# Three rounded products in place of one f32 product in the fill of a fused attention and two-layer expert kernel

## Chip, cores and metric

One core of one Trainium2 chip. The metric is the device time of the program in microseconds; three runs of the kernel before give a median of 1349.17 us (1349.16 to 1350.17).

## The reference, cut

```python
f = 1 / (1 + exp(-f_logit))                       # q, k, v, f_logit: (4, 8, 768, 48)
for t in range(768):                              # gated linear attention
    state = f[:, :, t, :, None] * state + k_t v_t^T
    y[:, :, t] = q_t . state
x = y as (3072, 384)
h = x @ w_in                                      # 384 -> 2048
g = (a0 + a1 h + a2 h^2 + a3 h^3) / (1 + |b0||h| + |b1| h^2 + 1e-6)
x = g @ w_out                                     # 2048 -> 384
out = sum over 4 experts e of p_e * (relu(x @ w1[e]) @ w2[e])   # 384 -> 1024 -> 384
```

## The kernel before

The 768 positions are cut into NCH = 6 chunks of 128; a chunk has NB = 4 batches, and a `Block` is one chunk of one batch of the attention (4 pairs of heads side by side). The first feed-forward layer is cut into NJ1 = 16 slots of 128 hidden columns; a slot has an input half (384 columns of `w_in`) and an output half (384 of `w_out`). The experts have 8 slots each.

All engines run instructions in the order in which the program lists them (a manual schedule), so that a waiting instruction holds everything listed behind it on its engine. SP issues nearly all DMAs, also in that order.

Three stretches follow each other.

**Start-up.** `Att.first(s, ...)` runs for rounds s = 0 to 4 (tau = -6 to -2). Round s prepares block (0, s): ScalarE's `exp`, VectorE's `w` (L437, f + 1, clipped), four `scans` (L444), ScalarE's `inverse` (L452, L453), `k_hat` (L458, GpSimd but for the first block), `newton1`, `newton2` and `q_hat` (L464, L468, L473), then its scores on TensorE. The same round ends the block before it (`old`): `k_copy`, `masked` (L488), products for y, and `x_hi` (L553), which copies the block's y from a bank to the tile `x` of chunk 0. In chunk 0, x is one f32 tile and `x_lo` does nothing. Between them stand conversions of the first slots: the slots of the first layer come as 64-bit words and `conv` makes f32 of them (L805, L806 on ScalarE, L808, L809 on VectorE, L812 an integer add, on VectorE for the first four slots and on GpSimd for the others). VectorE's list in rounds 1 and 2 is: w, scans, masked, newton1, newton2, q_hat, L808, L809, L812. ScalarE's in round 1: inverse, k_copy, L805, L806, exp of the next block, x_hi; in round 2 the exp stands ahead of L805.

**Fill.** Steps tau = 0 to 17 take chunk 0 through the first layer. Step tau has `fill_in(tau + 1)` (three f32 products, L961) and `fill_out(tau - 2)` (three f32 products, L969). An f32 product stands in the trace as two MATMUL records. `gate_step` makes the rational function between them: on VectorE L993, L1002 and L1012 of the slot before and L998, L1004 and L1019 of the new one, on ScalarE L982 to L984, L999 and L1000. The conversion of a later slot follows (L808, L809, then L812 on GpSimd). In steps tau = 0 to 3 `scale_state` (L581, two GpSimd products of 48 partitions) stands ahead of that step's L812. Each converted slot is stored whole to DRAM (`w1s`), to be used again for the chunks after.

**Main part.** From step v = -1 (v = tau - 19) the experts of chunk c run while chunk c + 1 goes through attention and the first layer. These products are "rounded": each f32 operand is split in a high part in fp32r and a low part, and three fp32r products (L910, L920) stand for one. A slot's half that is used for the first time is loaded raw, its high part made by ScalarE (L865), its low part by GpSimd or VectorE (L867), and if it is used again, both parts are stored (`scr`); from then on it is loaded split. For the 16 input halves of the first layer this first use is in steps v = 10 to 26, and the splits run about eight uses ahead. Block (1, 0) has its `q_hat` on GpSimd at the end of step v = -2.

Of the kernel before, what the change touches and what calls it, by code (L numbers as in the profile page):

```python
# [8 lines left out]
F32 = mybir.dt.float32  # L9
# [10 lines left out]
C = 128  # L20
# [386 lines left out]
class Block:  # L407
# [25 lines left out]
    def w(self):  # L433
        f = d = self.f[0:PR]
        if self.c > 1:
            d = self.d = self.py[0:PR].rearrange("p (r t) -> p r t", r=NP)
        self.nc.vector.tensor_scalar(d, f, 1.0, WLIM, ALU.add, ALU.min)  # L437

    def scans(self):
        self.g = self.att.p1.tile([128, NP, C], F32, tag="g", name="g")  # L440
# [28 lines left out]

    def q_hat(self):  # L470
        q = self.q[0:PR]
        eng = self.nc.gpsimd if self.c else self.nc.vector
        eng.tensor_tensor(out=q, in0=q, in1=self.i[0:PR], op=ALU.mult)  # L473

    def scores(self, r):
# [68 lines left out]
        self.nc.tensor.matmul(self.pa[0:PR, o:o + 2 * D], self.kt[:, r], self.v[:, o:o + 2 * D], start=True, stop=True)  # L544

    def x_part(self, i):
        x = self.att.x_of(self.c)
        x = x if self.c == 0 else x[:, i]
        return x[:, :, self.b * C:(self.b + 1) * C]

    def x_hi(self):
        xt = self.py[:, 0:DM].rearrange("p (m t) -> p m t", m=3)
        self.nc.scalar.copy(out=self.x_part(0), in_=xt)  # L553

    def x_lo(self):
        if self.c:
            xt = self.py[:, 0:DM].rearrange("p (m t) -> p m t", m=3)
            self.nc.vector.tensor_tensor(out=self.x_part(1), in0=xt, in1=self.x_part(0).bitcast(F32), op=ALU.subtract)

    def finish(self):  # L560
        nc = self.nc
# [22 lines left out]
class Att:  # L584
# [9 lines left out]

    def x_of(self, c):
        if c not in self.x:
            shape, dt = ([128, 3, 512], F32) if c == 0 else ([128, 2, 3, 512], F32R)
            self.x[c] = self.xp.tile(shape, dt, tag="x", name="x")
        return self.x[c]

    @staticmethod
# [21 lines left out]
        for _ in range(n):  # L623
            self.tc.nc.tensor.matmul(self.spare[:, 0:C], ident, ident, start=True, stop=True)

    def first(self, s, conv, fetch, ahead):

        new, old, nxt = (self.blocks.get((0, b)) for b in (s, s - 1, s + 1))
        rs = range(NP)
        if s == 0:  # L630
            new.exp()
            self.warm(WARM[0])
        if new:
            new.w()
            new.scans()
            new.inverse()
            new.k_hat()
        if s == 0:
            self.scalars()
        if old:  # L640
            old.k_copy()
        if nxt and s != 1:
            nxt.exp()
        for f in conv[0]:
            f()
        if s == 1:
            nxt.exp()
        if old:
            old.masked()
            for f in old.y_parts():  # L650
                f()
            for r in rs:
                old.update(r)
        if new:
            new.newton1()
            new.newton2()
            new.q_hat()
        if old:
            old.x_hi()
        if new:  # L660
            self.warm(WARM[1])
            for r in rs:
                new.scores(r)
            for r in rs:
                new.k_t(r)
            if nxt:
                self.warm(WARM[2 + s])
            else:
                ahead()
        if old:  # L670
# [45 lines left out]
    def early(self, blk, v):  # L716

        s = {}
        if blk.b == 0:
            s = {-4: {ACT0: [blk.exp]}, -3: {POST: [blk.w, blk.scans]},  # L720
                 -2: {POST: [blk.inverse, blk.k_hat, blk.newton1, blk.newton2, blk.q_hat]},
                 0: {PB: [blk.all_scores], REST: [blk.masked]},
                 1: {PB: 5 * [lambda: None] + [blk.keys_and_y] + 3 * [lambda: None], REST: [blk.k_copy, blk.x_hi]},
                 2: {PA: 4 * [lambda: None] + [blk.all_updates] + 4 * [lambda: None], DVE1: [blk.x_lo, blk.finish]}}
        if blk.b == 1:
            s = {-1: {ACT0: [blk.exp]}, 0: {DVE1: [blk.w], REST: [blk.scans]},
                 1: {ACT0: [blk.inverse], POOL1: [blk.k_hat], REST: [blk.newton1, blk.newton2, blk.q_hat]},
                 2: {REST: [blk.all_scores]}, 3: {**self.stage(blk, 5), DVE1: [blk.masked]},
                 4: {**self.stage(blk, 6), DVE1: [blk.x_lo, blk.finish], REST: []}}
        if blk.b == 2:  # L730
            s = {1: {ACT0: [blk.exp]}, 2: {DVE1: [blk.w], REST: [blk.scans]},
                 3: {ACT0: [blk.inverse], POOL1: [blk.k_hat], DVE1: [blk.newton1], REST: [blk.newton2, blk.q_hat]},
                 5: self.stage(blk, 5), 6: self.stage(blk, 6)}
            s[4], s[5] = {REST: [blk.all_scores]}, {**s[5], DVE1: [blk.masked]}
        return s.get(v, {})
# [17 lines left out]
def fused(ctx, tc, aps, consts, gm, big, dp, prep, flag_op):  # L753
# [18 lines left out]
    att.scalars = prep.scalars  # L772
    att.e0 = tp.tile([128, NB, NP], F32, tag="t", name="e0")

    w1s = [dp.tile([128, SW], F32, name=f"w1s{j}") for j in range(NJ1)]
    scr = {(i, h): dp.tile([128, 2, DM], F32, name=f"ws{i}_{h}") for i in range(NSLOT) for h in range(2)}
    prs = dp.tile([NCH * NB * NE, C], F32, name="prs")

# [16 lines left out]
    def conv(i, stage):  # L795
        if stage == 0:
            t = spare_pools[i % 3].tile([128, 2 * SW], F32, tag=("o", "s1", "pb")[i % 3], name="t")
            temp[i] = t
        f = temp[i]
        p, m = f[:, 0:SW], f[:, SW:2 * SW].bitcast(I32)  # L800
        pi = p.bitcast(I32)
        words = raw[i].rearrange("p (n w) -> p n w", w=2)
        lo, hi = words[:, :, 0], words[:, :, 1]
        if stage == 0:
            nc.scalar.activation(out=p, in_=hi.bitcast(F32), func=AF.Abs, scale=2.0 ** -112, accum_out=big[:, i:i + 1])  # L805
            nc.scalar.activation(out=m, in_=lo.bitcast(U32), func=AF.Identity, scale=2.0 ** -29)  # L806
        else:
            nc.vector.tensor_scalar(pi, pi, 3, None, ALU.logical_shift_left)  # L808
            nc.vector.scalar_tensor_tensor(out=pi, in0=hi, scalar=-2 ** 31, in1=pi, op0=ALU.bitwise_and, op1=ALU.bitwise_or)  # L809
            w1f[i] = wp.tile([128, SW], F32, tag="w", name="wf")  # L810
            eng = nc.vector if CONV1[i] < NB - 6 else nc.gpsimd
            eng.tensor_tensor(out=w1f[i].bitcast(I32), in0=pi, in1=m, op=ALU.add)  # L812
            late.append(partial(nc.sync.dma_start, out=w1s[i], in_=w1f[i]))
            if i % 2:
                late.append(fetch)

    late = []

# [16 lines left out]
    state = {"ready": 0, "split": 0, "used": 0, "vec": False}  # L835
    tile_of, raw_of, stores, seen = {}, {}, [], set()
    rawbuf = []
    again = {h for n, h in enumerate(uses) if h in uses[:n]}
    first_use = [h not in uses[:n] for n, h in enumerate(uses)]

    def make_ready(n):
        while state["ready"] < min(n, len(uses)):
            k = state["ready"]
            state["ready"] += 1
            i, h = uses[k]
            t = tile_of[k] = wp.tile([128, 2, DM], F32R, tag="w", name="w")
# [273 lines left out]
    for v in range(-FILL - 6, LAST + 1):  # L1120
# [282 lines left out]
```

## Time and profile before

| | |
|---|---|
| median of 3 runs | 1349.17 us |
| the profiled execution | 1348.14 us, of which span 1346.3 us |
| TensorE (PE) busy | 1322.1 us, 98% of the span |
| VectorE (DVE) busy | 906.0 us, 67% |
| ScalarE (ACT) busy | 666.2 us, 49% |
| GpSimd (POOL) busy | 280.3 us, 21% |
| mean granted TensorE clock | 0.998 |

The span runs from the first to the last instruction; 1.84 us of the profiled execution lie outside it. A busy share is a mean over stretches that have different limits, and the ends of matmuls are modelled, so that TensorE's share says little by itself. In a timeline a row has its start, its time, engine, line, operation, output<-inputs, and, in brackets, how long the engine sat idle before it and what released it. Rows of one line that follow each other are merged (x2, x4).

### The profile page before, as it was taken

Reading aid. Unit: us, or ns where it says so; the run is one execution under the profiler, and the core shown is the slowest. Engines: PE = TensorE matmul, PEld = TensorE weight load, DVE = VectorE, ACT = ScalarE, POOL = GpSimd, SP = SyncE. Lnnn points to the kernel's source line nnn. Section 1 sums busy time; section 2 is a strip of 40 time slices with the busy share of each in tenths; the row PEclk is TensorE's granted clock in tenths of the full one; section 3 lists DMA queues with packets and bytes.
Section 4 is the critical chain, followed back from the end, with each engine's and each line's share of the span. In section 5 each row is a group of like instructions: output and inputs, shape, how many; then the busy total and the mean of one; then the engine's idle time right before and its main releaser. Section 6 shows DMA issues by size and latency. Waiting matters only on the chain.

```text
span 1346.3 us, 19626 instructions
## 1 busy us (share of the span) xinstructions
PE 1322.1 (98%) x7180; PEld 1058.6 (79%) x7180; DVE 906.0 (67%) x1389; ACT 666.2 (49%) x1164; POOL 280.3 (21%) x235
## 2 busy tenths in 40 slices
PE   8998999999999999999999999999999999999998
PEld 7444888778788888888888888888888888888887
DVE  8999868998566776757665947676856565752221
ACT  5996557757355545445444525454535544421111
POOL 2333334576310122100120220010210010110010
PEclk9999999999999999999999999999999999999999
DMA  9638985767785665676666657666757666667660
GB/s 348 210 143 315 368 311 203 275 237 260 278 273 177 196 213 176 198 243 206 200 212 182 213 183 256 218 191 195 220 179 239 193 196 191 195 192 241 192 194 27
DMA packets 116855, 294.16 MB, mean 219 GB/s; under 512 B 13232, under 2 KB 28944, under 8 KB 115984
## 3 DMA queue, kind: packets, MB, share of 16 engines
q1 hardware_dynamic: 116320, 292.70, 66.8%
q8 instruction: 59, 0.97, 0.3%
q14 instruction: 44, 0.36, 0.1%
q10 hardware_dynamic: 432, 0.13, 0.0%
HBM read 243.98 MB, written 48.81 MB: 217 GB/s over the span
## 4 chain that ended last, share of the span: by engine, by line


## 5 line engine op out<-in xcount | busy, mean ns | idle before, releaser
L910 PE MATMUL bank<-x,w 128*128 128x512 f32 x2448 | 595.2, 392 | 5.7 <-DVE gl L1033 4.9
L910 PEld LDWEIGHTS bank<-x,w 128*128 128x128 f32 x2448 | 458.2, 188 | 103.7 <-DVE gl L1033 6.6
L920 PE MATMUL bank<-gh,w 128*128 128x512 f32 x1584 | 492.6, 392 | 0.8 <-DVE s L1091 0.8
L920 PEld LDWEIGHTS bank<-gh,w 128*128 128x128 f32 x1584 | 294.1, 188 | 66.4 <-issue 4.0
L920 PE MATMUL bank<-gl,w 128*128 128x512 f32 x792 | 308.6, 390 | 0.0
L1033 DVE SCALAR_TENSOR_TENSOR gl<-bank,gh 128x512 fp32r<-128x512 f32 x192 | 131.6, 685 | 136.1 <-ACT gh L1032 135.7
L1074 POOL TENSOR_TENSOR o<-o,t 128x512 f32<-128x512 f32 x64 | 92.4, 1470 | 535.0 <-DVE t L1067 535.0
L1032 ACT ACTIVATE gh<-bank 128x512 fp32r<-128x512 f32 x192 | 113.9, 594 | 121.1 <-PE bank L910 121.1
L920 PEld LDWEIGHTS bank<-gl,w 128*128 128x128 f32 x792 | 148.7, 188 | 31.2
L998 DVE SCALAR_TENSOR_TENSOR q<-q,sc,r 128x512 f32<-128x512 f32 x80 | 67.0, 837 | 141.5 <-ACT r L983 141.5
L1009 ACT CAST gh<-q 128x512 fp32r<-128x512 f32 x80 | 49.2, 615 | 162.6 <-DVE q L1007 162.5
L978 ACT COPY h<-bank 128x512 f32<-128x512 f32 x80 | 47.0, 588 | 112.9 <-PE bank L910 112.8
L867 POOL TENSOR_TENSOR w<-rawbuf,w 128x384 fp32r<-128x384 f32 x68 | 79.2, 1190 | 33.3 <-ACT w L865 27.4
L1024 DVE TENSOR_TENSOR gl<-q,gh 128x512 fp32r<-128x512 f32 x80 | 56.8, 710 | 32.8 <-ACT gh L1009 32.6
L1019 DVE SCALAR_TENSOR_TENSOR y<-y,sc,h 128x512 f32<-128x512 f32 x80 | 74.9, 936 | 2.8
L999 ACT ACTIVATE r<-q,sc 128x512 f32<-128x512 f32 x80 | 58.0, 725 | 27.3 <-DVE q L998 20.4
L993 DVE SCALAR_TENSOR_TENSOR q<-q,r 128x512 f32<-128x512 f32 x80 | 68.6, 857 | 0.1
L458 POOL TENSOR_TENSOR k<-k,g 112x512 f32<-112x512 f32 x23 | 34.4, 1496 | 153.7 <-DVE g L444 77.2
L984 ACT ACTIVATE y<-h,sc 128x512 f32<-128x512 f32 x80 | 64.2, 802 | 0.0
L1007 DVE SCALAR_TENSOR_TENSOR q<-y,sc,q 128x512 f32<-128x512 f32 x80 | 62.2, 777 | 1.8
L1000 ACT ACTIVATE r<-r 128x512 f32<-128x512 f32 x96 | 60.7, 632 | 3.0
L1091 DVE TENSOR_TENSOR s<-s,bank 128x512 f32<-128x512 f32 x45 | 30.1, 685 | 45.9 <-PE bank L920 45.8
(117 smaller groups left out, 1275.5 us busy)
## 6 DMA issues: line engine op xcount, KB each, us to landing
w<-ws SPq DMA_DIRECT2D x456, 384.0 KB, 3.5
ws<-w SPq DMA_DIRECT2D x96, 384.0 KB, 4.8
raw<-in_w_dram SPq DMA_DIRECT2D x16, 768.0 KB, 6.8
rawbuf<-in_w_dram SPq DMA_DIRECT2D x64, 192.0 KB, 4.8
v<-in_v_dram SPq DMA_DIRECT2D x24, 320.0 KB, 5.1
f<-in_qkf_dram SPq DMA_DIRECT2D x24, 256.0 KB, 3.9
k<-in_qkf_dram SPq DMA_DIRECT2D x24, 256.0 KB, 4.0
q<-in_qkf_dram SPq DMA_DIRECT2D x24, 256.0 KB, 4.5
```

The source lines that it names most:

```text
L867: eng.tensor_tensor(out=t[:, 1], in0=r, in1=t[:, 0].bitcast(F32), op=ALU.subtract)
L910: nc.tensor.matmul(ps, a[:, o], b[:, kk, :], start=(n == 0), stop=(n == 8))
L920: nc.tensor.matmul(acc[m], a[:, o], b, start=(start and n == 0), stop=(stop and n == last))
L984: nc.scalar.activation(out=y, in_=h, func=AF.Identity, scale=sc[:, 0:1], bias=sc[:, 1:2])
L993: vec.scalar_tensor_tensor(out=q0, in0=q0, scalar=QC, in1=r0, op0=ALU.add, op1=ALU.mult)
L998: vec.scalar_tensor_tensor(out=q, in0=q, scalar=sc[:, 5:6], in1=r, op0=ALU.mult, op1=ALU.add)
L1000: nc.scalar.activation(out=r, in_=r, func=AF.Exp, scale=-1.0)
L1007: vec.scalar_tensor_tensor(out=q0, in0=y0, scalar=sc[:, 3:4], in1=q0, op0=ALU.subtract, op1=ALU.mult)
L1019: vec.scalar_tensor_tensor(out=y, in0=y, scalar=sc[:, 2:3], in1=h, op0=ALU.subtract, op1=ALU.mult)
L1032: nc.scalar.activation(out=gh, in_=h, func=AF.Relu)
L1033: nc.vector.scalar_tensor_tensor(out=gl, in0=h, scalar=0.0, in1=gh.bitcast(F32), op0=ALU.max, op1=ALU.subtract)
L1074: add()
```

## The change

The first-layer input products of the fill become three rounded ones. For this the tile x of chunk 0 gets a high and a low part, so that `x_lo` (L558, a VectorE subtraction) now runs for the four blocks of chunk 0; and a new function `split_in(i)` splits the input half of slot i on GpSimd (a copy and a subtraction) and stores both parts. The later uses load the halves split, with no first-use split. Only the output half goes to `w1s`. Besides, `w` moves from VectorE to ScalarE for all 24 blocks, right behind `exp`, and the `q_hat` of block (1, 0) moves from GpSimd to VectorE.

```diff
     def w(self):
-        self.nc.vector.tensor_scalar(d, f, 1.0, WLIM, ALU.add, ALU.min)
+        self.nc.scalar.activation(out=d, in_=f, func=AF.Identity, bias=self.att.consts[0][0:PR, 8:9])
     def q_hat(self):
-        eng = self.nc.gpsimd if self.c else self.nc.vector
+        eng = self.nc.gpsimd if self.c and (self.c, self.b) != (1, 0) else self.nc.vector
     def x_lo(self):
-        if self.c:
-            xt = ...
-            self.nc.vector.tensor_tensor(out=self.x_part(1), in0=xt, in1=self.x_part(0).bitcast(F32), op=ALU.subtract)
+        xt = ...
+        self.nc.vector.tensor_tensor(out=self.x_part(1), in0=xt, in1=self.x_part(0).bitcast(F32), op=ALU.subtract)
     def first(self, s, conv, fetch, ahead, split):
         if s == 0:
             new.exp()
+            new.w()
         if new:
-            new.w()
             new.scans()
...
         if old:
             old.k_copy()
+        if s == NB - 1:
+            split(0)
         if nxt and s != 1:
             nxt.exp()
+            nxt.w()
         for f in conv[0]:
             f()
         if s == 1:
             nxt.exp()
+            nxt.w()
...
         if old:
             old.x_hi()
+            if not nxt:
+                old.x_lo()
...
         if old:
             old.finish()
+            if nxt:
+                old.x_lo()
         for f in conv[1]:
             f()
 # fused
+    def split_in(i):
+        h, l = win[i] = (g2p.tile(..., tag="gh"), g2p.tile(..., tag="gl"))
+        src = w1f[i][:, 0:DM]
+        nc.gpsimd.tensor_copy(out=h[:, 0:DM], in_=src)
+        nc.gpsimd.tensor_tensor(out=l[:, 0:DM], in0=src, in1=h[:, 0:DM].bitcast(F32), op=ALU.subtract)
+        for n, t in enumerate((h, l)):
+            late.append(partial(nc.sync.dma_start, out=scr[i, 0][:, n], in_=t[:, 0:DM].bitcast(F32)))
-    first_use = [h not in uses[:n] for n, h in enumerate(uses)]
+    first_use = [h not in uses[:n] and (h[0] >= NJ1 or h[1]) for n, h in enumerate(uses)]
     def fill_in(j, lo=0, hi=NB):
         for kk in range(3):
-            nc.tensor.matmul(ps[:, t], w[:, kk * 128:(kk + 1) * 128], att.x[0][:, kk, t], start=(kk == 0), stop=(kk == 2))
+            for a, b in ((wh, x[:, 0]), (wl, x[:, 0]), (wh, x[:, 1])):
+                nc.tensor.matmul(ps[:, t], a[:, o], b[:, kk, t], start=(n == 0), stop=(n == 8))
 # main loop, at the head of step tau
+        if 1 <= tau + 3 < NJ1:
+            split_in(tau + 3)
```

## Rows read from the trace of the kernel before

**Rows 1.** The windows: busy us (count) of PE, PEld, DVE, ACT, POOL; then clock, DMA.

```profile
60.00:80.00 20.00, 20.00 (x47) 8.41 (x46) 19.86 (x32) 18.05 (x31) 6.60 (x4) 1.00 0.65 236
...
200.00:300.00 100.00, 96.82 (x552) 78.31 (x551) 93.73 (x121) 69.30 (x127) 57.75 (x46) 1.00 0.68 239
304.00:308.00 4.00, 4.00 (x13) 3.09 (x12) 3.42 (x6) 3.85 (x8) 2.56 (x3) 0.57 1.01 369
1100.00:1120.00 20.00, 20.00 (x90) 16.57 (x89) 12.71 (x17) 6.21 (x11) 4.70 (x3) 1.00 0.60 184
```

**Rows 2.** The timeline of one fill step: start us, us, engine, line, operation.

```profile
59.62 0.75 DVE L998 SCALAR_TENSOR_TENSOR bank<-bank,sc,r 128x512 f32<-128x512 f32 x1
...
62.79 0.55 DVE L808 TENSOR_SCALAR t<-t 128x768 int32<-128x768 int32 x1
...
63.38 0.96 DVE L809 SCALAR_TENSOR_TENSOR t<-raw,t 128x768 int32<-128x768 int32 x1
...
64.48 1.83 POOL L812 TENSOR_TENSOR wf<-t 128x768 int32<-128x768 int32 x1 [3.38 <-DVE t L809]
...
64.86 0.75 DVE L998 SCALAR_TENSOR_TENSOR bank<-bank,sc,r 128x512 f32<-128x512 f32 x1
```

**Rows 3.** The timeline of start-up round 1, VectorE and ScalarE.

```profile
14.28 0.69 DVE L473 TENSOR_TENSOR q<-q,i 112x512 f32<-112x512 f32 x1
...
14.83 0.66 ACT L431 ACTIVATE f<-f 112x512 f32<-112x512 f32 x1
14.89 0.55 DVE L808 TENSOR_SCALAR t<-t 128x768 int32<-128x768 int32 x1
15.35 0.50 ACT L553 COPY x<-bank 128x384 f32<-128x384 f32 x1
```

**Rows 4.** The timeline of start-up rounds 2 and 4 and the first gate.

```profile
22.22 0.69 DVE L473 TENSOR_TENSOR q<-q,i 112x512 f32<-112x512 f32 x1
...
23.44 0.45 ACT L553 COPY x<-bank 128x384 f32<-128x384 f32 x1
...
33.73 1.28 DVE L488 TENSOR_TENSOR am<-bank,mask 128x512 f32<-128x512 f32 x2
...
36.22 0.48 ACT L553 COPY x<-bank 128x384 f32<-128x384 f32 x1 [1.81 <-PE bank L501]
...
39.22 0.76 DVE L998 SCALAR_TENSOR_TENSOR bank<-bank,sc,r 128x512 f32<-128x512 f32 x1 [0.35 <-ACT r L983]
```

**Rows 5.** The groups by line, 0 to 210 us: busy us, mean ns.

```profile
L437 DVE TENSOR_SCALAR f<-f 112x512 f32<-112x512 f32 x8 | 3.9, 488 | 3.4 <-ACT f L431 3.3
...
L558 DVE TENSOR_TENSOR x<-bank,x 128x384 fp32r<-128x384 f32 x4 | 2.2, 547 | 0.0
```

**Rows 6.** The timeline, GpSimd: memsets and subtractions of 384 elements.

```profile
0.73 1.48 POOL L612 MEMSET s<- 128x384 f32 x4 [0.29 <-POOLq L1390]
...
111.28 1.96 POOL L867 TENSOR_TENSOR w<-rawbuf,w 128x384 fp32r<-128x384 f32 x2 [2.40 <-ACT w L865]
```

**Rows 7.** The timeline, GpSimd and VectorE side by side, at 238 us.

```profile
238.37 3.50 DVE L993 SCALAR_TENSOR_TENSOR q<-q,r 128x512 f32<-128x512 f32 x1
238.37 4.37 POOL L867 TENSOR_TENSOR w<-rawbuf,w 128x384 fp32r<-128x384 f32 x4
```

**Rows 8.** The timeline of the q_hat of block (1,0) on GpSimd.

```profile
125.78 2.46 POOL L473 TENSOR_TENSOR q<-q,i 112x512 f32<-112x512 f32 x1 [3.15 <-DVE i L468]
```

**Rows 9.** The waits of TensorE from 122 to 400 us: in all, times, longest.

```profile
PE bank L910 <- DVE gl L1033: 4.9, 3, 1.8
PE bank L477 <- POOL q L473: 1.7, 1, 1.7
PE bank L493 <- DVE am L488: 1.5, 1, 1.5
PE bank L920 <- DVE s L1091: 0.8, 1, 0.8
PE bank L910 <- ACT h L978: 0.8, 1, 0.8
```

More of the change, by code (lines that the diff above doesn't have):

```diff
@@ L546, in x_part @@
     def x_part(self, i):
-        x = self.att.x_of(self.c)
-        x = x if self.c == 0 else x[:, i]
-        return x[:, :, self.b * C:(self.b + 1) * C]
+        return self.att.x_of(self.c)[:, i, :, self.b * C:(self.b + 1) * C]
     def x_hi(self):
@@ L555, in x_lo @@
     def x_lo(self):
-        if self.c:
-            xt = self.py[:, 0:DM].rearrange("p (m t) -> p m t", m=3)
-            self.nc.vector.tensor_tensor(out=self.x_part(1), in0=xt, in1=self.x_part(0).bitcast(F32), op=ALU.subtract)
+        xt = self.py[:, 0:DM].rearrange("p (m t) -> p m t", m=3)
+        self.nc.vector.tensor_tensor(out=self.x_part(1), in0=xt, in1=self.x_part(0).bitcast(F32), op=ALU.subtract)
     def finish(self):
@@ L596, in x_of @@
         if c not in self.x:
-            shape, dt = ([128, 3, 512], F32) if c == 0 else ([128, 2, 3, 512], F32R)
-            self.x[c] = self.xp.tile(shape, dt, tag="x", name="x")
+            self.x[c] = self.xp.tile([128, 2, 3, 512], F32R, tag="x", name="x")
         return self.x[c]
@@ L624, in warm, with first @@
             self.tc.nc.tensor.matmul(self.spare[:, 0:C], ident, ident, start=True, stop=True)
-    def first(self, s, conv, fetch, ahead):
+    def first(self, s, conv, fetch, ahead, split):
         new, old, nxt = (self.blocks.get((0, b)) for b in (s, s - 1, s + 1))
@@ L719, in early @@
         if blk.b == 0:
-            s = {-4: {ACT0: [blk.exp]}, -3: {POST: [blk.w, blk.scans]},
+            s = {-4: {ACT0: [blk.exp, blk.w]}, -3: {POST: [blk.scans]},
                  -2: {POST: [blk.inverse, blk.k_hat, blk.newton1, blk.newton2, blk.q_hat]},
@@ L725, in early @@
         if blk.b == 1:
-            s = {-1: {ACT0: [blk.exp]}, 0: {DVE1: [blk.w], REST: [blk.scans]},
+            s = {-1: {ACT0: [blk.exp, blk.w]}, 0: {REST: [blk.scans]},
                  1: {ACT0: [blk.inverse], POOL1: [blk.k_hat], REST: [blk.newton1, blk.newton2, blk.q_hat]},
@@ L730, in early @@
         if blk.b == 2:
-            s = {1: {ACT0: [blk.exp]}, 2: {DVE1: [blk.w], REST: [blk.scans]},
+            s = {1: {ACT0: [blk.exp, blk.w]}, 2: {REST: [blk.scans]},
                  3: {ACT0: [blk.inverse], POOL1: [blk.k_hat], DVE1: [blk.newton1], REST: [blk.newton2, blk.q_hat]},
@@ L773, in fused @@
     att.e0 = tp.tile([128, NB, NP], F32, tag="t", name="e0")
-    w1s = [dp.tile([128, SW], F32, name=f"w1s{j}") for j in range(NJ1)]
+    w1s = [dp.tile([128, DM], F32, name=f"w1s{j}") for j in range(NJ1)]
     scr = {(i, h): dp.tile([128, 2, DM], F32, name=f"ws{i}_{h}") for i in range(NSLOT) for h in range(2)}
@@ L809, in conv @@
             nc.vector.scalar_tensor_tensor(out=pi, in0=hi, scalar=-2 ** 31, in1=pi, op0=ALU.bitwise_and, op1=ALU.bitwise_or)
+            eng = nc.vector if CONV1[i] < NB - 6 else nc.gpsimd
             w1f[i] = wp.tile([128, SW], F32, tag="w", name="wf")
-            eng = nc.vector if CONV1[i] < NB - 6 else nc.gpsimd
             eng.tensor_tensor(out=w1f[i].bitcast(I32), in0=pi, in1=m, op=ALU.add)
-            late.append(partial(nc.sync.dma_start, out=w1s[i], in_=w1f[i]))
+            late.append(partial(nc.sync.dma_start, out=w1s[i], in_=w1f[i][:, DM:SW]))
             if i % 2:
                 late.append(fetch)
+    win = {}
+    def split_in(i):
+        h, l = win[i] = (g2p.tile([128, 512], F32R, tag="gh", name="gh"), g2p.tile([128, 512], F32R, tag="gl", name="gl"))
+        src = w1f[i][:, 0:DM]
[3 more added lines that the diff above has]
+            late.append(partial(nc.sync.dma_start, out=scr[i, 0][:, n], in_=t[:, 0:DM].bitcast(F32)))
     late = []
@@ L853, in make_ready @@
                 seen.add(k)
-                src = w1s[i] if i < NJ1 else w2[i - NJ1]
-                nc.sync.dma_start(out=r, in_=src[:, h * DM:(h + 1) * DM])
+                src = w1s[i] if i < NJ1 else w2[i - NJ1][:, h * DM:(h + 1) * DM]
+                nc.sync.dma_start(out=r, in_=src)
             else:
@@ L958, in fill_in @@
     def fill_in(j, lo=0, hi=NB):
-        w, ps, t = w1f[j], (banks[3], banks[4], banks[7])[j % 3], slice(lo * C, hi * C)
+        (wh, wl), ps, t = win[j], (banks[3], banks[4], banks[7])[j % 3], slice(lo * C, hi * C)
+        x, n = att.x[0], 0
         for kk in range(3):
-            nc.tensor.matmul(ps[:, t], w[:, kk * 128:(kk + 1) * 128], att.x[0][:, kk, t], start=(kk == 0), stop=(kk == 2))
+            o = slice(kk * 128, (kk + 1) * 128)
+            for a, b in ((wh, x[:, 0]), (wl, x[:, 0]), (wh, x[:, 1])):
+                nc.tensor.matmul(ps[:, t], a[:, o], b[:, kk, t], start=(n == 0), stop=(n == 8))
+                n += 1
         if hi == NB:
             gate_queue.append((0, j, ps))
+            win.pop(j)
     def fill_out(j):
@@ L1127, in fused @@
             prep()
+        if 1 <= tau + 3 < NJ1:
+            split_in(tau + 3)
         if tau + 6 <= NB:
-            att.first(tau + 6, conv_ops(tau), fetch, partial(fill_in, 0, 0, NB - 1))
+            att.first(tau + 6, conv_ops(tau), fetch, partial(fill_in, 0, 0, NB - 1), split_in)
         run_late()
```

## The prediction

> **What bounds the kernel now.** I read the page first. TensorE is busy for 1322.1 of 1346.3 us, VectorE for 906.0, so the page alone says "TensorE, everywhere". But the change is nearly all in the first 122 us and in some waits up to 350 us, and those stretches have limits of their own. So the second view was the windows. In the middle of the fill TensorE is busy for 20.00 of 20 us, VectorE for 19.86, ScalarE for 18.05 [rows 1]: two engines are full at once, and the windows can't say which one leads.
>
> The third view, the timeline of one fill step, can. L998 comes at 59.62 and again at 64.86: a step is 5.24 us [rows 2]. TensorE has 47 records in 20.00 us [rows 1], 0.426 us each, and twelve in a step (three f32 products in, three out, two records each): 5.11 us. VectorE's eight operations of a step follow each other with no idle time on any of their rows. So VectorE sets 5.24 us, and TensorE follows 0.13 us behind it in price. The reader is to see that a TensorE at 100% may still be the follower.
>
> In start-up VectorE leads too: in round 1 q_hat (L473) starts at 14.28, L808 at 14.89, with nothing between [rows 3]. In the late main part TensorE does lead: 90 records in 20.00 us, while VectorE and ScalarE have room (the last of [rows 1]). Between them, from 122 to 400 us, the waits view gives TensorE's stalls: 4.9 us for L1033 in three waits, 1.7 us for the q_hat of block (1, 0), 1.5 us for L488 and two of 0.8 us [rows 9]. VectorE is busy for 93.73 of the 100 us from 200 on [rows 1].
>
> **The products.** An f32 product is two records of 0.426 us; a rounded one, by 90 records in 20.00 us, is 0.222 us. Input products of a slot: 6 x 0.426 = 2.56 us before, 9 x 0.222 = 2.00 after; 16 slots give 9.0 us of TensorE's time. I book none of it. VectorE's step has the same eight operations before and after, so its 5.24 us stay and TensorE only waits longer. If the cover were gone (TensorE leading), at most 5.24 to 4.55 us a step could be had.
>
> **x_lo in start-up: the main cost.** Four new subtractions of 0.547 us (L558 [rows 5]) on the engine that leads. Worse is where they stand. In rounds 1 and 2 VectorE's list becomes q_hat, x_lo, L808, L809, L812, then the next block's scans; x_lo waits for x_hi, which ScalarE reaches late, and now later by the w that stands ahead of it. Price of w on ScalarE: not shown as such; the exp of the same shape takes 0.66 us [rows 3], taken for both ends.
>
> Round 1, by the clock of before: q_hat ends at 14.97; x_hi ends at 15.35 + 0.50 + 0.66 = 16.51; x_lo ends near 17.06, and L808, which started at 14.89, can start there: +2.1 us, less the 0.49 us of w that VectorE is rid of (L437, mean of eight [rows 5]): +1.6. Round 2: q_hat ends at 22.91, x_hi at 23.44 + 0.45 + 0.66 = 24.55: a wait of 1.64, plus x_lo, less w: +1.65. Round 3 has no exp or w ahead of x_hi, and x_lo hardly waits: +0.2. Round 4: masked ends at 35.01, x_hi at 36.70 after waiting for TensorE [rows 4]; x_lo stands between masked and L808: 1.7 + 0.5 = +2.2. Round 0, where w follows exp and nothing covers it: +0.2. Sum 5.85. Behind it VectorE had waited 0.35 us for the first gate [rows 4]; that much is absorbed. **+5.5 us** when the fill gets going. Both ends for the range: 3.9, if ScalarE's w hides in its other waits in rounds 1 and 2 (0.66 less in each, 0.3 in the rest), and 6.5, if the late scores of a round put off the next masked as well. As VectorE leads from there on, nothing in the fill gives it back.
>
> **split_in.** The subtraction of 384 elements takes 0.98 us on GpSimd; its copy isn't in the trace. Below, a memset of that size (0.37 us), above, the subtraction itself (0.98) [rows 6]; I take 0.5, nearer to the memset because it too has one stream less. In the steady fill L812 starts at 64.48, 0.14 us after L809 ends, and takes 1.83 us [rows 2]; copy and subtraction follow: done 3.5 us after L809's end. The next L808 comes 5.24 - 0.96 - 0.59 = 3.69 us after it. So GpSimd is just done, and has time to spare.
>
> That matters, since the two engines disturb each other: L993 takes 3.50 us beside four L867 of GpSimd [rows 7], while L998, with an operand in a bank, takes 0.75 us beside L812 in every step [rows 2]. The Trainium skill ("GPSIMD Engine Reference", Key points) says that GpSimd shares its SBUF interfaces with VectorE and contends with VectorE instructions that have two SBUF inputs or run in a two-port mode. The trace agrees, with 3.50 us. By that rule L808, L809 and the Newton steps are exposed and the gate is not.
>
> Where they do meet: in round 3 the splits of slots 0 and 1 (3 us of GpSimd) meet L464, L468 and L473. Bounds: nothing, and 2.8 us (3.50 - 0.69, the row of L993); I take 0.9. In steps 1 to 3 scale_state's two products now stand behind the split; at about 0.5 us each (an estimate: half a subtraction, by elements) they end 4.5 us after L809 and reach 0.8 us into L808 and the next L809. The pair at 238 us cost VectorE 2.8 us in 4.37, or 0.64 a us, so 0.5 a step; I take half, as L808 is short, 0.8 in all. In step -1 the split of slot 3 meets prep: 0.2; SP's queue holds the loads of the main part behind the last split's stores at the fill's end, 0.2. **+2.1 us.**
>
> **q_hat of block (1, 0).** On GpSimd it took 2.46 us and TensorE waited 1.7 for it [rows 8, 9]. On VectorE it takes 0.69 (the row of L473 in [rows 3]) and starts where GpSimd's did. TensorE gets back 1.7, and the 0.7 us that VectorE's queue gains behind it is covered by w, which leaves (0.488 twice): **-1.4 us**, some lost again.
>
> **The main part.** Sixteen first-use splits go: each 0.5 us of ScalarE (not shown here as a row; I take the copy L553, 0.45 to 0.50, same size [rows 3, 4]) and 0.98 us or more of GpSimd beside a VectorE that is 94% busy; some 14 of them lie between 165 and 305 us. w leaves VectorE for 20 blocks, 0.5 to 0.7 us each, and enters ScalarE at 69% [rows 1]. DMA bytes are the same in sum: 0.39 MB of stores move into the fill, where there is room. What can be won is bounded by TensorE's stalls: 4.9 + 1.5 + 0.8 + 0.8 = 8.0 us, and the half-speed stretch behind one of them (clock 0.57 from 304 to 308 us, 13 records in 4 us, where 18 would go by at 0.222 each: about 1.2 us) [rows 1, 9]. Below: nothing, if the stalls only move. Splits are about a third of what crowds GpSimd there, so I take a little over a third: **-3.4 us**.
>
> **Sum.** 5.5 + 2.1 - 1.4 - 3.4 = +2.8. The profiled execution took 1348.14 us (span 1346.3 and 1.84 around it), so 1350.9; it lies 1.03 below the median of the runs, and by that median I predict **1352.0 us**. What a measurement can tell from no change I take as 0.2%, 2.7 us.
>
> **Rivals.**
> *A, forecast:* VectorE's stalls in start-up cost 7 to 8 us, the main part gives back some 5: 1352.0, own range 1349.5 to 1355. Chance 0.45.
>
> *B, the other side:* the stalls from 122 to 400 us all go. Price 1.7 + 8.0 + 1.2 = 10.9 against 5.5 + 1.0 (half of the meetings): -4.4, 1344.8 us. It decides from the point where more than 10 of the 10.9 come back against the full 7.6, or 9 against these 6.5, or where the fill's step falls below 5.24. For it: all of these waits end with VectorE or GpSimd, which are relieved. Against it: L1033 still stands behind Newton steps and scans. Chance 0.13.
>
> *C, they cancel:* x_lo costs its 6 us, and the main part gives back 6 of 10.9: 1349. For it: the two sums are of one size. Chance 0.24.
>
> *D, GpSimd's copy is dear:* at 0.98 us the pair ends 4.0 us after L809, beyond L808's start at 3.69. Each of eleven steps with a conversion then loses 0.3 to 0.6 us, 3 to 6 us more: 1356.5. For it: the sharing that the row of L993 shows. Against it: L808 is short. It decides once the copy takes over 0.7 us. The skill's page has this contention as a rule, as said above. Chance 0.18.
>
> That the change doesn't shorten the fill at all, though it takes 9 us from TensorE, is part of A, C and D.
>
> **Chances.** Slower by over 0.2% (over 1351.9): half of A and more (0.28), all of D, a little of C: 0.49. Faster: B and a little of C: 0.15. Same: 0.36. Range: B's better half and D's worse half left out: 1346.0 to 1357.5.
>
> **What would show it.** In the profile after: x_lo (L558) with idle time before it, released by ScalarE's x_hi, near 1.5 us in rounds 1, 2 and 4; the first gate's L998 near 45 us in place of 39.22; steps of the middle fill still 5.24 us, with TensorE idle about 0.6 us in each and waiting for VectorE; L808 at its 0.55 us (A) or longer (D); TensorE's wait of 1.7 us gone; the sum of its waits from 122 to 400 us lower by a third (A), or near nothing (B). I am wrong if steps get shorter than 5.1 us, or if x_lo doesn't wait.

## The result, and the profile after

The changed kernel takes 1357.9 us (median of 6 runs, 1356.9 to 1360.4) against 1349.4 for the kernel before (6 runs, 1349.2 to 1350.6): a ratio of 1.0066, with a 95% interval of 1.0055 to 1.0076. That is 8.9 us slower by the ratio, where 2.8 us were forecast. The profiled execution of after is its slowest, 1360.41 us (span 1358.3), 2.5 us above its median, so differences read from its trace are somewhat too large. Prices below come from ratios where a run gives one.

Start-up first. The rows are from the timeline of after; L555 is x_lo, L551 x_hi, L437 w (they answer to [rows 3 to 5]).

```profile
14.17 0.69 DVE L473 TENSOR_TENSOR q<-q,i 112x512 f32<-112x512 f32 x1
...
15.96 0.72 ACT L437 ACTIVATE f<-f,sc 112x512 f32<-112x512 f32 x1
16.59 0.46 ACT L551 CAST x<-bank 128x384 fp32r<-128x384 f32 x1
...
17.08 0.56 DVE L555 TENSOR_TENSOR x<-bank,x 128x384 fp32r<-128x384 f32 x1 [2.22 <-ACT x L551]
17.56 0.55 DVE L812 TENSOR_SCALAR t<-t 128x768 int32<-128x768 int32 x1
...
26.61 0.56 DVE L555 TENSOR_TENSOR x<-bank,x 128x384 fp32r<-128x384 f32 x1 [1.73 <-ACT x L551]
...
41.88 0.56 DVE L555 TENSOR_TENSOR x<-bank,x 128x384 fp32r<-128x384 f32 x1 [1.71 <-ACT x L551]
...
47.07 0.75 DVE L1017 SCALAR_TENSOR_TENSOR bank<-bank,sc,r 128x512 f32<-128x512 f32 x1
```

x_lo makes VectorE wait 2.2, 1.7 and 1.7 us for ScalarE in rounds 1, 2 and 4, and the first gate comes at 47.07 us in place of 39.22 [rows 4]. The rounded products don't make that good: the middle of the fill still steps by 5.23 us, as before [rows 2].

```profile
78.79 0.75 DVE L1017 SCALAR_TENSOR_TENSOR bank<-bank,sc,r 128x512 f32<-128x512 f32 x1
...
81.96 0.56 DVE L812 TENSOR_SCALAR t<-t 128x768 int32<-128x768 int32 x1
...
84.02 0.75 DVE L1017 SCALAR_TENSOR_TENSOR bank<-bank,sc,r 128x512 f32<-128x512 f32 x1
```

Gate 12 is at 110.19 (before 101.49: 8.7 us late, where the forecast's 5.5 and 1.9 make 7.4). Then come the last steps. In the timeline of after, SPq is SP's DMA queue, L826 and L827 are the split of slot 15, the last, on GpSimd; L879 (ScalarE) and L881 (GpSimd) are first-use splits for the main part:

```profile
111.62 2.00 POOL L881 TENSOR_TENSOR w<-rawbuf,w 128x384 fp32r<-128x384 f32 x2
...
113.54 0.52 POOL L826 CAST gh<-wf 128x384 fp32r<-128x384 f32 x1
...
114.09 0.32 SPq L835 DMA_DIRECT2D ws<-gh  x1
114.14 1.00 POOL L827 TENSOR_TENSOR gl<-wf,gh 128x384 fp32r<-128x384 f32 x1
...
115.17 0.32 SPq L835 DMA_DIRECT2D ws<-gl  x1
...
115.58 0.88 SPq L887 DMA_DIRECT2D ws<-w  x2
...
116.51 0.50 SPq L869 DMA_DIRECT2D rawbuf<-in_w_dram  x1
...
121.66 1.00 ACT L879 CAST w<-rawbuf 128x384 fp32r<-128x384 f32 x2 [3.02 <-DMA rawbuf<-in_w_dram]
...
123.28 0.63 ACT L1019 ACTIVATE r<-r 128x512 f32<-128x512 f32 x1
...
123.95 0.70 DVE L1012 SCALAR_TENSOR_TENSOR bank<-bank,r 128x512 f32<-128x512 f32 x1 [2.67 <-ACT r L1019]
...
127.69 8.10 PE L988 MATMUL bank<-g,wf 128*128 128x512 f32 x12 [4.18 <-DVE g L1031]
...
135.22 1.96 PE L924 MATMUL bank<-x,w 128*128 128x512 f32 x6
```

Read it as a chain. GpSimd comes to the split of slot 15 only behind L881. The stores of gh and gl are issued 0.03 us after GpSimd has written each; all that SP has to issue waits behind them. The load of raw weights goes out at 116.51, 6.3 us after gate 12. In before nothing held it, and it went out 4.0 us after gate 12:

```profile
105.44 0.48 SPq L855 DMA_DIRECT2D rawbuf<-in_w_dram  x1
```

ScalarE waits 3.0 us until this load has landed, and behind its split stand the Ln and Exp of the gate (L1018, L1019); VectorE waits 2.7 us for those, TensorE 4.2 us for VectorE. Gates 14 and 15 lie 7.0 us apart (before 3.9). And it isn't over when TensorE has its data, as the windows of after show (columns as in [rows 1]):

```profile
60.00:80.00 20.00, 18.76 (x59) 10.58 (x58) 19.86 (x30) 17.79 (x31) 14.01 (x15) 1.00 0.78 263
...
124.00:126.00 2.00, 0.00 (x0) 0.00 (x0) 1.61 (x3) 2.00 (x4) 0.20 (x1) 1.00 0.84 248
126.00:128.00 2.00, 0.31 (x1) 0.31 (x2) 2.00 (x4) 1.94 (x4) 0.00 (x0) 0.57 1.03 409
128.00:130.00 2.00, 2.00 (x3) 0.86 (x3) 1.85 (x4) 0.17 (x1) 0.00 (x0) 0.50 1.06 369
```

After the idle stretch the granted clock is 0.50, 1.2 GHz, and the last twelve records of out products take 8.10 us (5.71 in m5 below). The first main product starts at 135.22, before at 121.87: 13.35 us late. The q_hat of block (1, 0) gives back 0.9 of it (12.47), and the rest of the main part 1.2: the end is 11.3 us late.

### The profile page after: what moved, and what is told of

Read it like the earlier page. It is cut to its first block, busy times and chain, and to the rows that moved or that the text cites. A ratio compares the mean times of both kernels' runs of the same rounds, so it can differ in the third digit from the quotient of the medians.

```text
span 1358.3 us, 19771 instructions
## 1 busy us (share of the span) xinstructions
PE 1321.9 (97%) x7231; PEld 1070.6 (79%) x7231; DVE 885.4 (65%) x1368; ACT 676.2 (50%) x1172; POOL 284.1 (21%) x252
## 4 chain that ended last, share of the span: by engine, by line
## 5 line engine op out<-in xcount | busy, mean ns | idle before, releaser
L1052 DVE SCALAR_TENSOR_TENSOR gl<-bank,gh 128x512 fp32r<-128x512 f32 x192 | 131.6, 685 | 141.2 <-ACT gh L1051 140.8
L1017 DVE SCALAR_TENSOR_TENSOR q<-q,sc,r 128x512 f32<-128x512 f32 x80 | 62.5, 782 | 148.7 <-ACT r L1002 148.7
L881 POOL TENSOR_TENSOR w<-rawbuf,w 128x384 fp32r<-128x384 f32 x54 | 60.3, 1141 | 44.6 <-ACT w L879 41.8
L1018 ACT ACTIVATE r<-q,sc 128x512 f32<-128x512 f32 x80 | 58.0, 725 | 21.3 <-DVE q L1017 13.8
L1019 ACT ACTIVATE r<-r 128x512 f32<-128x512 f32 x96 | 60.7, 633 | 3.0
## 6 DMA issues: line engine op xcount, KB each, us to landing
f<-in_qkf_dram SPq DMA_DIRECT2D x24, 256.0 KB, 4.2
k<-in_qkf_dram SPq DMA_DIRECT2D x24, 256.0 KB, 4.7
q<-in_qkf_dram SPq DMA_DIRECT2D x24, 256.0 KB, 4.9
```

The source lines that it names most:

```text
L881: eng.tensor_tensor(out=t[:, 1], in0=r, in1=t[:, 0].bitcast(F32), op=ALU.subtract)
L1017: vec.scalar_tensor_tensor(out=q, in0=q, scalar=sc[:, 5:6], in1=r, op0=ALU.mult, op1=ALU.add)
L1019: nc.scalar.activation(out=r, in_=r, func=AF.Exp, scale=-1.0)
L1052: nc.vector.scalar_tensor_tensor(out=gl, in0=h, scalar=0.0, in1=gh.bitcast(F32), op0=ALU.max, op1=ALU.subtract)
```

## The experiments

Theory 1, formed from the two traces: VectorE leads the fill, so that the wait for x_hi, GpSimd's share and, at the fill's end, SP's order are paid in full, and the products give nothing. Its rivals: w on ScalarE is the loss; the half clock is a cause of its own; the last conversion is late by GpSimd's and VectorE's work, whatever SP does.

Ratios are to the kernel before, run beside each; 0.1% is 1.35 us, and a difference of two ratios is sure to some 2 to 3 us by their intervals, so that the smaller gains below (e2, t1, e4) can't be told from nothing by the time alone. "First product" is the start of the main part's first product, in us behind before's 121.87; gates count from 0. Both are read from one execution of each run. Four runs with the same start-up (after, e4, t1, e7) have their first gate between 45.77 and 47.07, so differences of gates are good to about 1.3 us.

| run | median us | ratio, interval | first gate | first product |
|---|---|---|---|---|
| after | 1357.9 | 1.0066 (1.0055 to 1.0076) | 47.07 | +13.35 |
| e1_xlo_behind | 1354.9 | 1.0044 (1.0027 to 1.0061) | 42.64 | +8.59 |
| e2_stores_behind | 1356.4 | 1.0057 (1.0040 to 1.0074) | 46.59 | +10.47 |
| e3_w_on_vector | 1366.7 | 1.0127 (1.0110 to 1.0144) | 51.41 | +19.7 |
| e4_qhat_on_pool | 1357.6 | 1.0056 (1.0040 to 1.0073) | 46.77 | +13.45 |
| t1_last_stores_late | 1355.9 | 1.0051 (1.0035 to 1.0068) | 46.33 | +7.13 |
| e6_stores_late_xlo_behind | 1353.3 | 1.0033 (1.0021 to 1.0046) | 43.63 | +5.00 |
| m3_f32_products | 1350.1 | 1.0006 (0.9996 to 1.0016) | 41.48 | +3.61 |
| e3b_w_on_vector_old_places | 1358.4 | 1.0070 (1.0054 to 1.0087) | 46.85 | +12.15 |
| e7_stores_on_gpsimd | 1352.9 | 1.0029 (1.0018 to 1.0041) | 45.77 | +7.96 |
| m4 (m3 and e7) | 1348.7 | 0.9990 (0.9980 to 0.9999) | 41.68 | +3.88 |
| m5 (m3, last stores on GpSimd) | 1346.9 | 0.9984 (0.9974 to 0.9993) | 40.95 | +1.76 |
| e9 (e1, last stores on GpSimd) | 1349.6 | 1.0004 (0.9995 to 1.0014) | 42.63 | +4.01 |
| m6_w_and_qhat_alone | 1345.9 | 0.9978 (0.9966 to 0.9989) | 38.91 | -0.66 |

**x_lo.** e1 moves x_lo of rounds 1, 2 and 4 behind the next block's second conv step:

```
-            if not nxt:
+            if s == NB - 1:
                 old.x_lo()
...
-            if nxt:
-                old.x_lo()
         for f in conv[1]:
             f()
+        if old and s != NB - 1:
+            old.x_lo()
```

> The changed kernel with x_lo of start-up rounds 1, 2 and 4 moved behind the conversion (L812, L813, L816). Theory 1 (VectorE leads, and x_lo's waits for x_hi of 2.22, 1.73 and 1.71 us stand in its way): the first gate's L1017 comes 5 us sooner than 47.07 us, the time falls by about 5 us, from 1357.9 to 1352.5-1353.5. Theory 2 (it is w on ScalarE that delays start-up, wherever x_lo stands): less than 1.5 us is won, 1356.5 or more. Theory 3 (the stretches at half clock cost the time, and VectorE's waits only show beside them): no gain beyond the scatter, 1357-1360.

The first gate comes 4.4 us earlier, and 3 us of that reach the end, short of the 5 expected. Gates 14 and 15 stay 7.2 us apart: the fill's end is a trouble of its own.

m3 takes the rounded products and x_lo of chunk 0 away and leaves the splits, w and q_hat:

```
-            for a, b in ((wh, x[:, 0]), (wl, x[:, 0]), (wh, x[:, 1])):
-                nc.tensor.matmul(ps[:, t], a[:, o], b[:, kk, t], start=(n == 0), stop=(n == 8))
-                n += 1
+            nc.tensor.matmul(ps[:, t], w[:, kk * 128:(kk + 1) * 128], att.x[0][:, kk, t], start=(kk == 0), stop=(kk == 2))
```

> The changed kernel with the products of the fill left as they were before (three f32 ones; x of chunk 0 in one f32 part, so x_lo of chunk 0 is gone); the splits in the fill and their stores, w on ScalarE and q_hat on VectorE stay. Theory 1 (x_lo's waits on the leading VectorE are the loss in start-up, and the 9 us that the rounded products save are worth nothing): first gate near 40 us instead of 47, steps 5.24 us, the fill's end still late by SP's queue; 1352 to 1354. Rival (the rounded products do hide something): steps longer than 5.24 us, or 1358 and more.

The first gate comes 5.6 us earlier, the steps stay 5.23 us, and the time is that of before within 0.16%, under both ends of what was expected. So the rounded products hid nothing. x_lo costs 5.6 us of start-up by these two executions, 4.1 by e7 and m4 below.

**w and q_hat.** e3 puts w back on VectorE, but at its new places, ahead of other work:

```
-        self.nc.scalar.activation(out=d, in_=f, func=AF.Identity, bias=...)
+        self.nc.vector.tensor_scalar(d, f, 1.0, WLIM, ALU.add, ALU.min)
```

> The changed kernel with w on VectorE again for all 24 blocks. Theory 1: x_hi comes 0.7 us sooner in rounds 1 and 2, but VectorE has 0.45 us more in rounds 1 to 3; nearly even in start-up, 0 to 1.5 us less there, and up to 1 us more in the main part: 1356.5-1359. Theory 2 (w on ScalarE is what delays start-up): 3 us or more less, under 1355.

It comes out 8.2 us slower than after, outside both expectations. This was no clean undo: VectorE then waits for ScalarE's exp, and 4.3 us are lost at the first gate. It shows only how dear a wait on the leading engine is. e3b puts w at its old places as well (`new.w()` behind `if new:`, DVE1 and POST in the schedule):

> The changed kernel with w on VectorE at the places that it had in the kernel before; all else as changed. Theory 1 (x_lo waits for ScalarE's x_hi, of which w ahead of it is 0.72 us in rounds 1 and 2; VectorE pays about as much for w itself): first gate 46 to 47.5 us, 1357 to 1358.5. Theory 2 (w on ScalarE is the main loss): first gate below 44 us and the time below 1355.

It is as after. x_lo waits less in rounds 1 and 2 (1.08 and 1.00 us), but VectorE then does w itself (0.42 us each), and the first gate is only 0.2 us earlier, no difference that can be told. e4 undoes the q_hat:

```
-        eng = self.nc.gpsimd if self.c and (self.c, self.b) != (1, 0) else self.nc.vector
+        eng = self.nc.gpsimd if self.c else self.nc.vector
```

> The changed kernel with the q_hat of block (1, 0) on GpSimd again. Theory 1 (it gave back 0.9 us, as the start of the products shows: 13.35 us late before it, 12.47 after): 1358.5-1359. Rival (on VectorE it delays the relu's low part L1052 by as much as it wins): no change, 1357.5-1358.

TensorE waits 0.7 us for GpSimd's q_hat, and the run can't be told from after. From the first product to the 60th of the main part, after gains 0.9 us on before and e4 0.5, so the move itself is worth 0.3 us or so here. m6 has the two parts alone, in the kernel before:

> The kernel before with two parts of the change alone: w on ScalarE at its new places, and q_hat of block (1, 0) on VectorE. No split in the fill, f32 products, no x_lo in chunk 0. If w costs start-up nothing (theory 1: it moves between two engines that wait for each other), first gate 39 to 40 us, and what is left of the 2.3 us are GpSimd's splits; 1347 to 1349. If w is what delays start-up, first gate 41 us or more, and 1350.

It has the lowest time of all, 3.0 us under before and below what was expected (m5, below, is level with it by the intervals). Its first gate is 0.3 us earlier, and it is 1.6 us ahead by the main part's 60th product. The rest comes after that, up to 400 us, though TensorE's waits from 122 to 410 us change places more than they shrink: 9.6 us, before 9.7 [rows 9]. The half-clock stretch of [rows 1] is gone, but not the wait of 1.8 us in front of it, so nothing shows that the two moves took it away.

```profile
PE bank L912 <- DVE gl L1035: 5.5, 4, 1.8
PE bank L493 <- DVE am L488: 1.3, 2, 0.9
PE bank L922 <- ACT gh L1011: 1.2, 1, 1.2
```

**The fill's end.** Four ways to keep SP's loads from standing behind GpSimd's splits. e2 issues the stores at the end of each step, t1 those of the last three slots after the last step of the fill, e7 lets GpSimd issue all of them, m5 and e9 only the last three slots':

```
-            late.append(partial(nc.sync.dma_start, out=scr[i, 0][:, n], in_=...))
+            parts.append(...)          # e2: all; t1: i >= NJ1 - 3
+            nc.gpsimd.dma_start(out=scr[i, 0][:, n], in_=...)   # e7, m4: all; m5, e9: i >= NJ1 - 3
...
+        for f in parts: f()            # e2: end of each step; t1: if tau == NJ1
```

> The changed kernel with the stores of split_in issued at the end of each step, behind the step's raw loads. Theory 1 (at the end of the fill SP waits for the last split's parts, and the loads behind it come late; ScalarE's cast then holds the gate of slot 14): ScalarE's wait of 3.02 us, VectorE's of 2.67 and TensorE's of 4.18 go, with the half clock after them; 4 to 5 us less, 1353-1354. Rival (the loads are late because the DMA engines carry more bytes there): the wait stays, 1357-1359.

Gates 14 and 15 are 5.7 us apart, so 1.3 of the 3.1 us come back there, not the 4 to 5 expected. The stores still stand ahead of the next step's loads.

> The changed kernel, with the stores of the split parts of the last three slots (13 to 15) issued after the last step of the fill, not at once; nothing else is moved. Theory 1 (SP's queue: the last loads stand behind stores that wait for GpSimd's split, ScalarE and VectorE wait for them, TensorE idles 4 us and runs at half clock behind it): gate 14 to 15 falls from 7.0 us to about 4 as before, the half-clock stretch near 126 us goes, and the time falls by 3.5 to 4.5 us, to about 1353.5. Rival (the last conversion is late by the work of GpSimd and VectorE itself, whatever SP does): gate 14 to 15 stays at 5.7 or more as with all stores behind the loads, and the time is 1356 to 1357.

Here gates 12 to 15 are 3.9 to 4.0 us apart, and the first product is 6.2 us earlier than in after. Yet only 2.0 us remain at the end, where 3.5 to 4.5 were expected: the six stores put off (L1236) now stand ahead of the next load, and that load, issued at 129.74, is the one for which ScalarE then waits 3.2 us. The timeline of t1 (its L870 to L1053 are after's L869 to L1052):

```profile
127.35 0.32 SPq L1236 DMA_DIRECT2D ws<-gl  x1
...
129.74 0.37 SPq L870 DMA_DIRECT2D rawbuf<-w1s  x1
...
136.66 0.51 ACT L880 CAST w<-rawbuf 128x384 fp32r<-128x384 f32 x1 [3.19 <-DMA rawbuf<-w1s]
...
137.70 0.69 DVE L1053 SCALAR_TENSOR_TENSOR gl<-bank,gh 128x512 fp32r<-128x512 f32 x1
...
138.45 3.77 PE L925 MATMUL bank<-x,w 128*128 128x512 f32 x9 [3.60 <-DVE gl L1053]
```

> The one before, and x_lo of rounds 1, 2 and 4 moved behind the next block's second conv step, as in the run e1_xlo_behind. If the two costs add up: first gate near 42.6 us as in that run, the first product of the main part near 126 us (4 behind before), and the time 1349.5 to 1351, the same as before within what can be told. If the end of the fill takes back what the start-up gains, 1353 to 1355.

The two gains add up: 4.5 us by the ratios, of 3.0 and 2.0. It misses the expected time by what t1 lost as well: 2.6 us go again between the first product (5.0 behind) and the 60th (7.6).

> The changed kernel, with the stores of all split parts issued by GpSimd, right behind its own split, and not by SP. Theory 1 (the loads of the main part stand in SP's queue behind stores that wait for GpSimd): gates 13 to 15 at 3.9 us each as before, first product of the main part about 8.7 behind before in place of 13.35, and, unlike with the stores put off to the fill's last step, no new late load behind it: 1353 to 1354. Rival (issuing costs GpSimd so much that the splits come late, or the loads are late by the traffic itself): gate 14 to 15 above 5.5 us, 1356 and more.

As theory 1 has it: gates 12 to 15 are 3.9 to 4.0 us apart, no half clock at the fill's end, 5.0 us faster than after by the ratios. The bytes are the same, so it was the place in the queue and not the traffic. The traces split the gain: from gate 12 to the first product after takes 25.0 us and e7 19.6. Of these 5.4 us, 3.0 lie between gates 14 and 15, and 2.4 are the price of the half clock, in the last twelve out records (8.10 for 5.71 us). There is a price in the first steps, as the timeline of e7 shows:

```profile
55.29 0.74 DVE L1017 SCALAR_TENSOR_TENSOR bank<-bank,sc,r 128x512 f32<-128x512 f32 x1
...
58.24 1.01 POOL L827 TENSOR_TENSOR gl<-wf,gh 128x384 fp32r<-128x384 f32 x1
58.46 1.21 DVE L812 TENSOR_SCALAR t<-t 128x768 int32<-128x768 int32 x1
59.19 0.59 POOL L829 DMA_DIRECT2D ws<-gh  x1
...
61.48 0.74 DVE L1017 SCALAR_TENSOR_TENSOR bank<-bank,sc,r 128x512 f32<-128x512 f32 x1
```

GpSimd is busy for 0.54 to 0.95 us with each issue (half of them under 0.56), so scale_state and the splits reach further into VectorE's conv, and the step is 6.19 us (after 5.72). The Trainium skill ("SBUF — State Buffer", SBUF: two separate sides) says that a DMA issued from GpSimd's queue has its descriptors made on GpSimd's cores, and advises ScalarE's or SP's queue where VectorE's work keeps GpSimd from making them. The issue times agree with the first. No run here shows the case of the advice; where SP's queue would wait for GpSimd's own result, e7 is the faster by 5.0 us.

> The two edits m3 and e7 together: f32 products and no x_lo in the fill, split parts stored by GpSimd; what stays of the change is the split in the fill, w on ScalarE and q_hat on VectorE. If the costs of theory 1 add up, start-up and the fill's end are within 2 us of before, and the main part's gain of 1 to 3 us decides: 1347.5 to 1350. If theory 1 misses a cost, 1351 and more.

> The run m3 (f32 products, no x_lo in chunk 0), with the stores of the split parts of the last three slots alone issued by GpSimd. If the long early steps of m4 came from GpSimd's issuing and the late end of m3 from SP's waits, this one has both right: early steps 5.7 us, gate 14 to 15 at 3.9 us, first product of the main part about 2.5 behind before (3.9 and 3.6 in the others), 1347 to 1348.5. If not, as m4: 1348.5 to 1350.

m4 has the long early steps (up to 6.18 us), m5 not (5.71), and m5 is 3.0 us faster than m3 by the ratios (1.3 of it lie between gate 12 and the first product in the traces). In the timeline of m5, with the last splits' stores on GpSimd (L837), the load that after issues 6.3 us behind gate 12 goes out 3.8 us behind it, at 107.79, and TensorE waits 1.06 us at full clock (its L1021 is after's L1017, L992 is L988):

```profile
107.79 0.46 SPq L877 DMA_DIRECT2D rawbuf<-in_w_dram  x1
...
108.86 0.56 POOL L837 DMA_DIRECT2D ws<-gh  x1
...
111.91 5.51 PE L992 MATMUL bank<-g,wf 128*128 128x512 f32 x12
...
111.92 0.76 DVE L1021 SCALAR_TENSOR_TENSOR bank<-bank,sc,r 128x512 f32<-128x512 f32 x1
...
115.83 0.76 DVE L1021 SCALAR_TENSOR_TENSOR bank<-bank,sc,r 128x512 f32<-128x512 f32 x1
...
118.48 5.71 PE L992 MATMUL bank<-g,wf 128*128 128x512 f32 x12 [1.06 <-DVE g L1035]
```

> The changed kernel, with rounded products, x_lo of rounds 1, 2 and 4 behind the next block's second conv step, and the stores of the last three slots' split parts on GpSimd. If the costs add up: first gate 42.6 to 43.6 us, first product of the main part 4 to 5 behind before, main part 2 to 3 us faster: 1350 to 1351.5. If it lands within 0.5 us of the like run with f32 products, the rounded products cost nothing once x_lo is out of the way.

e9, with rounded products and both repairs, is level with before, and 2.7 us slower than m5: that is what the rounded products and their x_lo cost with x_lo moved, 5.3 us with x_lo where the change has it (e7 against m4). x_lo is still on VectorE's list, and 1.7 of the 2.7 us lie before the first gate (42.63 for 40.95).

**Who leads the fill.** d1 and d2 leave VectorE's y times h out of the gate (and that factor out of the result), in before and in after; each is one run.

```
-        if new and not late:
-            vec.tensor_tensor(out=y, in0=y, in1=h, op=ALU.mult)
```

> The kernel before without the second product (y times h) of the Newton step in the fill's gate; this leaves that factor out of the result, and takes one VectorE operation of about 0.6 us out of each full step. If VectorE leads before's fill by only 0.13 us a step (the prediction's step), TensorE takes over at once: steps of 5.24 us fall to about 5.11, and the end comes 1 to 2 us earlier (near 1347.5). If TensorE's input products are free of any bound (VectorE leads by much), steps fall to about 4.6 and the end comes 6 us earlier.

> The changed kernel without the same VectorE product (that factor is left out of the result). If VectorE leads its fill and the 9 us that the products give back to TensorE are only waited away, the step of 5.24 us falls to about 4.6 (TensorE's own price now is some 4.55), 11 steps give 6 to 7 us, and the time is near 1351. If something else holds the step (GpSimd's split, SP's queue), the step stays above 5.1 and the time above 1355.5.

d1 takes 1347.15 us, d2 1356.02. The step of before falls to 4.77 to 4.84 us, that of after only to 5.06. In the timelines of d1 (L1010) and d2 (L1029), VectorE:

```profile
78.23 0.69 DVE L1002 SCALAR_TENSOR_TENSOR bank<-bank,r 128x512 f32<-128x512 f32 x1
79.03 0.75 DVE L1010 SCALAR_TENSOR_TENSOR g<-y,sc,bank 128x512 f32<-128x512 f32 x1
...
80.35 0.55 DVE L808 TENSOR_SCALAR t<-t 128x768 int32<-128x768 int32 x1
```

```profile
82.38 0.69 DVE L1021 SCALAR_TENSOR_TENSOR bank<-bank,r 128x512 f32<-128x512 f32 x1
83.17 0.75 DVE L1029 SCALAR_TENSOR_TENSOR g<-y,sc,bank 128x512 f32<-128x512 f32 x1
...
83.85 1.00 POOL L827 TENSOR_TENSOR gl<-wf,gh 128x384 fp32r<-128x384 f32 x1
84.49 0.78 DVE L812 TENSOR_SCALAR t<-t 128x768 int32<-128x768 int32 x1
```

Two things are to be seen. g now starts 0.79 or 0.80 us behind the operation that writes its input, where neighbours without that tie start 0.59 to 0.66 apart: leaving 0.6 us out shortens the list by 0.4. And in d2 GpSimd's subtraction reaches into L812, 0.78 us for 0.55. A faster VectorE runs into GpSimd's split, so in the changed fill less is to be had than the prediction's "5.24 to 4.55 us a step".

## Why the prediction was wrong

The step that failed is in split_in: "SP's queue holds the loads of the main part behind the last split's stores at the fill's end, 0.2". The wait was named and priced at almost nothing; it costs 5.0 us (after against e7; 5.4 in the traces, 2.4 of them half clock), 3.0 us with f32 products (m3 against m5). It was mis-sized because the chain behind it was not followed: the load feeds a split on ScalarE, the split stands ahead of a gate, the gate feeds TensorE, and in after TensorE's idle time is followed by half clock. The other steps:

- **VectorE leads the fill, and the products' 9 us are worth nothing:** right; steps of 5.23 us, and m3 loses nothing without them. But TensorE's price of a step was too high: 0.426 us a record was a stretched figure, as TensorE, waiting, showed itself busy all the time. d1 has steps of 4.77 us, so twelve records cost 0.398 each or less.
- **x_lo in start-up, +5.5:** right; 4.1 to 5.6 at the first gate, 5.3 of time. By the start of VectorE's conv in rounds 1 to 4 (L812 in after, L808 in before), after falls behind by 2.7, 1.6, 0.3 and 2.9 us, meetings with the splits included: round 1 cost 1.1 more than booked, as its wait was 2.2 us and the w that VectorE is rid of came back as 0.11 us only (q_hat at 14.17 for 14.28). Part of that wait is this execution's: ScalarE's exp waited 0.43 us for a load, and in e7, with the same start-up, x_lo waits 1.3 us in round 1.
- **split_in's meetings, +1.9:** the copy takes 0.50 us as booked (1.04 and 0.96 for the first two, in start-up); m5 is 2.8 us behind m6 at gate 12 (104.01 and 101.17), 2.0 of it before the first gate. Steps 1 to 3 lose 0.48 us each, the 0.5 of which half was taken.
- **q_hat, -1.4:** 0.9 us in after, 0.3 of it its own.
- **The main part, -3.4:** 2.9 us in e7 (from 7.07 to 4.19 behind), 2.8 in m5; 1.2 in the profiled after. w alone gives 1.4 of it (m6). The 1.7 us between e7 and after are the clock: in both TensorE idles for 1.09 and 0.58 us near 250 us, for a first-use split, but only in after do 3.4 us at half clock follow (256.0 to 259.3). So the estimate was near, and a single execution can miss it by that much (m5 has such a stretch too, but not the later loss). Later after loses 1.4 us again (9.9 behind at the main part's 900th product, 11.3 at the end), 1.2 of it is lost in e7 too, and the cause was not followed. The "0.39 MB of stores" are one slot's; sixteen slots move 6.3 MB into the fill.

With these sizes the sum is 5.3 + 2.8 + 5.0 - 0.9 - 2.9 = 9.3 us, against 8.9 by the ratio; as some of the terms are sure to 2 us only, so close a match is in part luck. Rival D stood nearest to the time, at 1356.5, but not by its mechanism: the copy takes 0.50 us, not 0.98, and steps from 4 on lose nothing. B and C fell with the fill's end.

After and m3 differ at the fill's end (4.65 and 0.6 us later against before than at gate 12), though SP's list is the same in both. From m3, its load (SP's queue) and two of its waits:

```profile
110.82 0.51 SPq L873 DMA_DIRECT2D rawbuf<-in_w_dram  x1
```

```profile
PE bank L988 <- DVE g L1031: 2.5, 1, 2.5
ACT w L883 <- DMA rawbuf<-in_w_dram: 1.7, 2, 1.3
```

The load goes out 6.3 us behind gate 12, just as in after. But it lands sooner: ScalarE waits 1.3 us, not 3.0, and gates 14 and 15 are 5.3 us apart, not 7.0. That is 1.7 of the 4.1 us. The other 2.4 are the half clock, which does not follow TensorE's 2.5 us of idle time in m3. Why the load lands later in after stays open.

## What to carry to other kernels

When a step moves, follow every queue that it is put into to the end: a store that waits for a slow engine holds all loads behind it, and those may feed an engine two steps further on. Repair it by the place in the queue (here, letting the engine that writes the data issue its last stores), and look again, for the stall may only have moved, as in t1. And try the small parts of a change alone: w and q_hat by themselves gained 3.0 us, while the part that was to free 9 us of TensorE, with its x_lo, splits and stores, cost all of the loss, since TensorE did not lead there.

## What was not expected of the hardware

- Half clock after idle time, but not by its length alone. TensorE idle for 4.2 us in after was followed by 6.8 us at 1.2 GHz, and 2.2 us of idle time near 54 us by 3.4 us. Yet 2.5 us in m3 at the fill's end were followed by none. In all thirteen runs of the table that have the fill's splits (all but m6), TensorE idles 1.09 and 0.57 to 0.59 us near 250 us; 3.4 us at half clock follow in after, e1, e3, e4, e3b, m3, m4, m5 and e9, none in e2, t1, e6 and e7. Such a stretch costs up to 1.7 us, by chance as far as these runs tell. At half clock an out product takes twice the time, 0.85 us a record.
- SP's issues, 0.32 to 0.5 us mostly, take up to 1.5 us near the fill's end (two in 2.51 us at 119.55 in after); in before too (1.40 at 114.31).
- VectorE's L812, with one input, slows down too beside GpSimd: 0.56 us alone, 0.78 beside the subtraction (d2), 0.84 to 0.85 beside scale_state (after), 1.21 beside the subtraction and an issue (e7).
